# Every matmul of a convolution-and-token-mixing kernel as a 64 by 64 array quarter

## The chip, the cores and the metric

The kernel runs on one core of a Trainium2 chip. The metric is the device time of one execution in microseconds (us). Inputs and output are float32 in device memory; inside the core the matmul operands are bfloat16.

## The reference

There are eight batches of 4224 tokens with 192 features. A causal convolution with seven softmax-normalised taps, one set of taps for each of eight heads of 24 features, makes `y`; then a token mixer without softmax follows.

```python
w = softmax(weight, axis=-1)                       # 8 heads x 7 taps
y[b, s, h, :] = sum_k w[h, k] * x[b, s - 6 + k, h, :]
wq, wk = y @ w_q, y @ w_k                          # 192 -> 64
W_tok = (1 / 8) * einsum("bsd,btd->bst", wq, wk)
mixed = einsum("bst,btd->bsd", W_tok, y)
out = relu(mixed) @ w_out                          # 192 -> 192
```

Since nothing non-linear stands between `wq`, `wk` and `mixed`, the kernel never forms the 4224 by 4224 matrix. It uses mixed = wq (wk' y) / 8 and wk' y = w_k' (y' y), so that per batch it needs the Gram matrix y' y (192 by 192), a 64 by 192 matrix M = w_k' (y' y) / 8, and mixed = wq M.

## The kernel before, in words

Everything is unrolled. Each step is an object of class `Op` with the engines that may run it, its emitter, what it `needs`, and the accumulator (PSUM) banks that it fills or drains. `Planner.plan` reads a written-out order, the string `PLAN`: `118F4` is operation 118 on TensorE in full-array mode into bank 4, `A` is ScalarE, `D` VectorE, `G` GpSimd, `S` SyncE. `Program.place` then gives each engine its operations in that order and works out the semaphore waits. So the order on each queue, the engine that drains each bank, and the bank are set by hand in `PLAN`; there is no scheduler on the chip. Seven banks are dealt out to steps; bank 7 (`GB`) holds the Gram matrix.

Per batch the steps are these, with the lines that the profile names:

- Load (`gen_load`, L513): GpSimd issues DMAs that read x as float32 and write it as bfloat16 into `XW`. A chunk is 128 tokens, of which 122 are new: each chunk repeats the six tokens before it, so that the convolution of a chunk is one product with a 128 by 128 band matrix. `XW` holds all eight batches, and all loads are issued without waiting for the compute.
- Convolution (`gen_conv`): band matrix of one head times up to 18 chunks x 24 features, by `halves` either as one 128 by 128 matmul (L315) or as two 128 by 64 ones (L316, L317). ScalarE or VectorE copies the bank to `Y` as bfloat16 (L621).
- Turning `Y` (`gen_transpose` L321 to L323, `gen_transpose_hi` L678), drained by VectorE into `YTL` (L648) and `YTH` (L688).
- Queries (`gen_wq`, L707 and L711), drained into `WQT` (L728).
- Gram (`gen_gram`, L744): three matmuls per chunk with a 64-column weight, in the upper and lower half of the columns of the array.
- Weights of the mix (`gen_mix_weights`, L763, L807), and then per block of 512 + 512 tokens the mix (`gen_mix`, L836, L848, L856), a relu into `RT` (L873, L874), the product with `w_out` (`fin` L902, `fin_other` L920), the copy to `OUT` (L941) and the store by SyncE (L949).

The three ways of splitting the array are called `COL2` (two tiles of 128 rows by 64 columns), `ROW2` (64 by 128) and `FULL`. The second half of batch b (mix, product, store) is interleaved in `PLAN` with the first half of batch b + 1. The stationary operand of each matmul is loaded by an instruction of its own, so each matmul of the program is two instructions of TensorE (PE and PEld in the profile).

```python
# gen_load, a full part: n chunks of 128 tokens, 122 apart
XW[:, b, full[0] : full[0] + n, :],
bass.AP(x_t, base + (CW * full[0] - KC + 1) * D, [[D, 128], [CW * D, n], [1, D]]),
# gen_gram, one chunk
for p, r, z, o, st in ((0, 0, D, 0, begin), (64, 64, D, 64, begin), (64, LO, D, 0, False)):
    mm = e.matmul(bank(GB)[p : p + 64, o : o + z - r], Y[0:w, yb, c, r : r + 64], Y[0:w, yb, c, r:z], ...)
# halves, unless the mode is FULL
e.matmul(out[0:64], lhsT[:, 0:64], rhs, **k)
return e.matmul(out[64:128], lhsT[:, 64:128], rhs, **k)
```

Of the kernel before, what the change touches and what calls it, by code (L numbers as in the profile page):

```python
# [6 lines left out]
ALU = mybir.AluOpType  # L7
# [5 lines left out]

PLAN = """
1D 38G 2D 13G 37G 39G 40G 8D 19D 41G 42G 9D 56G 57G 14D 58G 59G 60G 61G 62G 63G 5D 64G 15P 65G 12D 66G 67G
68G 69G 70G 71G 72G 73G 74G 0S 22D 75G 20D 76G 77G 78G 23D 24D 25A 16P6 6D 79G 80G 21D 11D 81G 26D 27D 17P
4D 28D 18A 29D 30P5 7D 33P6 34D 35D 31A 32A 36P 84F4 85D 90F3 91A 88P1 89D 86P5 87A 116P5 142P 94P2 95D 92F1
93A 96F3 43S 98F6 99A 97D 118F4 117D 106F5 102F1 104F3 82G 100F6 143P 107D 144P 3D 105A 103A 101D 145P 83G
110F5 108F6 109A 112F3 113A 111D 119D 114F0 120F1 115A 126P2 127D 130P6 131D 47A 124F0 48A 125D 46A 44S
122F5 128P2 146P 10D 147P 121D 49A 140P4 53A 50A 132P0 123D 138P3 129D 134P2 141D 148A 149P6 52A 133A 159P4  # L20
157P0 150D 45S 51A 151F6 135A 139D 160A 155F2 158D 161F4 154A 153A 152A 222P6 136P0 162A 137A 211P1 156D
171P4 197P 54A 224A 167P2 168A 213D 165P5 172D 169P0 198P 170A 166D 221P3 210P5 163P0 199P 55A 173F2 223D
225P3 212A 217P5 164A 214P0 226P 174D 179F2 218F 180D 219D 215F 227A 177F2 178D 244F4 175F3 216A 220S 181P5
264P0 233P6 202P 176D 243P2 246A 265A 182D 228P4 232P0 245A 235D 229P 254P6 256A 201P 234A 262P2 230D 231S
185P6 186D 263A 268P4 266P0 267A 200P 255P6 269D 195P3 187P2 196A 203D 239P4 236P0 257D 258P6 240F 188A 241A
183P3 184D 204F2 205A 237F 259F 247P4 250P2 248F 251F 238A 242S 260D 261S 249A 270F0 271A 189P6 190A 304P
276P4 277A 274P0 206P6 252D 253S 272P2 305P 191P4 208A 207A 209A 328P5 275D 273A 317P0 192D 330A 288P2 289D
290P3 278P4 279D 193P5 194D 318F6 329F2 319A 286F0 340F1 280F4 320A 321P5 331A 291D 332P2 287D 342A 335P0
322P 323A 281D 333P 336P 337A 309P 292P4 284F5 334D 338S 324P2 339P0 361P6 363A 325F 293D 282F4 341A 351P6
285D 298P5 353A 326D 327S 373P0 371P2 283D 306P 374A 302P4 303A 294P6 295A 375P0 299D 372D 300P5 301D 369P2  # L30
296P4 297D 362P6 307P 376A 343P0 350P4 370A 346P2 344P 364A 385F6 347F 352A 345D 308P 310D 357P0 348A 349S
365P4 354P2 358P 386D 311F5 312D 355F 356D 359A 360S 387F6 388D 313F5 316A 315A 366F 377F0 383F2 314A 447P5
411P 425P6 378A 384D 379P0 380D 367A 368S 449A 381P3 427A 436P2 438D 412P 424P5 435P0 382A 397P3 395P4 398D
389F2 426A 428P5 396D 431P3 437A 429P 432P 458P0 390D 430A 414P 460A 457P1 459A 442P5 433D 434S 439P3 415P
440F 441A 443F 444D 445S 446P1 468P0 413P 476P3 482P5 470A 448A 399P0 393P1 416P 469P2 483A 417A 477D 400D
478F3 453P5 471A 479A 394D 450P0 418F2 419D 454F 455A 451F 480F3 391F2 409P5 452A 456S 481D 401P6 402A 464P0
461P3 465P 466A 472P6 462P 392D 403P2 410D 463D 467S 492P5 493D 488P0 489A 518P 490P3 404D 407P5 491A 484P0
408D 485D 405P2 486P3 487A 406D 520P 494P5 495D 420P1 421A 423A 506P0 504P2 502P3 422A 531P4 505D 473F 554F1
496F2 507D 543F0 474D 475S 503D 533A 497D 532F6 500F5 556A 519P 516P2 542P3 545A 534D 535P0 501D 538P5 536F
537A 517D 539F 565F2 567A 544D 546P3 549P0 547P 550P 575P2 577A 540D 541S 548D 585P5 508P2 551A 552S 564P3  # L40
586D 553P0 555A 509D 523P 587P5 588A 522P 589P0 590A 566D 521P 576P6 583P4 578A 560P2 557P0 524D 525F6 526D
561F 558F 527F6 584A 562A 498F5 530A 579P4 559D 563S 528A 571P2 568P0 572P 580P 529A 573A 569P 499D 514P5
515A 512P6 513A 570D 574S 591P2 593P0 594A 581D 582S 639P5 510P4 599P6 592D 511D 600D 638P2 640A 595P0 601P4
602D 596A 641A 625P 597P2 650P6 652A 627P 660P0 642P4 661F6 598D 607F2 605F3 606D 662A 608D 643P 644D 663A
649P0 651A 626P 609P6 645P2 656P0 653P4 610D 646P 647D 648S 657P 654P 682P6 655D 684D 630P 658A 659S 628P
694P2 695A 613P0 603P1 683P6 690P4 691A 696P2 614D 611P0 629P 685A 604D 623P1 697A 692P4 693A 672P6 612D
617P0 615P3 624D 674D 671P1 618A 664P5 686P4 631D 632F0 616D 673A 665F 666A 706F3 633D 634F0 637A 687P 688A
689S 675P1 667P5 635A 707D 678P3 676P 636A 668P 669D 670S 679P 757P0 759D 732P 677A 702P1 700P5 680A 681S
701D 746P3 748A 619P0 620D 734P 756P3 758D 703A 745P5 733P 698P0 621P2 708P3 709D 747A 704P5 699A 622A 768P4
760P0 705A 752P2 761P 762A 770D 749P5 753P 710F4 711D 750F 779F1 781D 714P0 715D 754A 736P 720P2 763P3 778P0  # L50
751A 755S 767P5 780A 721D 764P 789P2 737P 791D 769D 735P 801P0 716P2 765A 766S 730P3 797P5 738D 718P4 731D
717D 790P3 802A 739P0 719D 712P1 713D 722P2 723D 798A 792A 740A 799P5 800A 803P3 771P0 793P2 772P 773A 774P5
804D 775P 782P3 776A 777S 785P0 783P 794P 795D 796S 786P 805P5 839P 784A 726P2 809P3 806D 787A 788S 811P0
810A 727D 724P5 813P6 814D 812A 807P3 728P2 815P0 816D 808A 725A 741P1 742A 821P6 822D 825P3 826D 823P4 744A
743A 853P1 729A 864P0 866A 852P5 854A 863P2 824D 855D 840P 875P0 877A 841P 827P4 859P5 865D 867P2 856P0 868P
860P 869A 857P 828D 886P4 861D 842P 870P2 874P5 858A 862S 876A 871P 896P0 897P1 888D 843P 817P4 885P5 872D
873S 878P2 898A 899A 881P0 879P 818D 837P4 838D 844P 887A 880A 819P6 829P5 845D 846P2 847A 892P3 820D 882P
900P6 893P 830D 831P2 848P5 883A 884S 833P0 832A 851A 901P 849A 894D 889P1 850A 904P4 906A 890P 905P3 907A
834D 917P0 902D 903S 835P6 891D 895S 928P4 930A 919D 908P2 916P0 909P 910A 911S 836D 929F6 931A 912P4 918D
913P 924P0 914A 915S 920P2 925P 926A 927S 941F6 943D 921F 932P4 953P0 955D 952P6 933P 922A 923S 940P2 942A  # L60
936P0 954D 937P 956P6 957P 934D 935S 944P2 945F 948P4 949P 938A 939S 958D 959S 946A 947S 950A 951S
""".split()

COL2, ROW2, FULL = "128x64", "64x128", "128x128"


class Op:


    n = 0  # L70

    def __init__(self, engines, emit, ns, needs=(), after=(), banks=0, drains=None, vt=0.0, mode=COL2, tail=0.0, whole=False):
        self.engines = (engines,) if isinstance(engines, str) else tuple(engines)
        self.emit = emit

        self.ns = ns
# [7 lines left out]
        self.vt = vt  # L84
        self.mode = mode

        self.whole = whole
        self.tail = tail
        self.users = 0
        self.bank = None  # L90
        self.engine = None
        self.end = None

        self.lands = 0.0

        self.size = 0
        Op.n += 1
        self.id = Op.n


class Planner:

    ENGINES = {"P": "PE", "F": "PE", "A": "ACT", "D": "DVE", "G": "POOL", "S": "SP"}

    def __init__(self, nbank):
        self.ops = []
        self.order = []
        self.nbank = nbank
# [8 lines left out]
    def plan(self):  # L117
        drains = {}
        for op in self.ops:
            if op.drains is not None:  # L120
                drains.setdefault(op.drains.number, []).append(op)
        users = [[] for _ in range(self.nbank)]
        place = {}
        for turn in PLAN:
            number, engine, bank = re.fullmatch(r"(\d+)([PFADGS])(\d*)", turn).groups()
            op = self.ops[int(number)]
            op.engine = self.ENGINES[engine]
            if engine == "F":
                assert op.whole
                op.mode = FULL  # L130
            assert op.engine in op.engines and op.number not in place
            if op.banks:
                op.bank = int(bank)
                for i in range(op.bank, op.bank + op.banks):
                    op.needs += users[i]
                    users[i] = drains[op.number]
            assert all(x.number in place for x in op.needs + op.after)
            place[op.number] = len(self.order)
            self.order.append(op)
# [892 lines left out]
```

## Time and profile before

| what | value |
|---|---|
| runs of the kernel before | 169.85, 170.89 and 171.77 us, median 170.89 |
| span of the profiled execution, first to last instruction | 168.6 us |
| TensorE (PE) busy | 158.3 us, 2874 matmuls |
| weight loads (PEld) | 116.1 us, 2882 |
| ScalarE (ACT), VectorE (DVE) | 123.8 us in 207, 116.2 us in 201 |
| granted TensorE clock | 0.994 |
| device memory read and written | 27.56 MB and 25.95 MB |

The profiled execution's own time is not listed beside its span; the three timed runs lie 1.3 to 3.2 us above that span, and their median 2.3 us. Busy time of TensorE counts a matmul until its modelled end, so that several matmuls overlap in it; weight loads run beside matmuls. A line such as `L744 PE MATMUL ps<-y 122*64 122x192` is a matmul with a weight of 122 rows by 64 columns that streams 192 columns. The shares of the DMA queues are of the time of 16 engines; two packets in flight on one engine count twice, so that they can add to more than 100%.

### The profile page before, as it was taken

What the parts mean: (1) busy time and instruction counts of PE and PEld (TensorE: products, weight loads), DVE (VectorE), ACT (ScalarE), POOL (GpSimd) and SP (SyncE); (2) the same over time, 40 slices, a digit from 0 to 9 for tenths busy, and PEclk for the clock granted to TensorE, in tenths of its full rate; (3) what the DMA queues carried; (4) which work ended last, traced back from release to release, by engine and by line L of the source; (5) the groups of instructions that cost most, each with busy time, mean ns of one, the idle gap of its engine ahead of it and who ended that gap; (6) DMA issues with size and microseconds to landing.
All of it is one profiled execution on the core that took longest, in us unless ns stands there. A gap on an engine that the chain in (4) does not pass through costs nothing.

```text
span 168.6 us, 6398 instructions
## 1 busy us (share of the span) xinstructions
PE 158.3 (94%) x2874; PEld 116.1 (69%) x2882; DVE 116.2 (69%) x201; ACT 123.8 (73%) x207; POOL 30.3 (18%) x39
## 2 busy tenths in 40 slices
PE   6978999999999999999999999999999999999980
PEld 1458846876677886777865867787778777884640
DVE  5745878774678777566999686875957758578640
ACT  3233699798977869888566978578897889568970
POOL 7999553530503120000000000000000000000000
PEclk9999999999999999999999999999999999999997
DMA  2999999999999999999999999996644463095897
GB/s 23 172 190 185 205 191 196 189 241 301 263 328 208 300 268 276 299 251 317 284 287 199 289 282 341 235 273 232 231 176 190 189 257 149 0 368 218 315 363 283
DMA packets 48154, 40.31 MB, mean 239 GB/s; under 512 B 37632, under 2 KB 40960, under 8 KB 48128
## 3 DMA queue, kind: packets, MB, share of 16 engines
q0 software_dynamic: 36128, 13.61, 67.6%
q1 hardware_dynamic: 12000, 26.31, 43.1%
q8 instruction: 22, 0.36, 0.8%
q14 instruction: 4, 0.03, 0.1%
HBM read 27.56 MB, written 25.95 MB: 317 GB/s over the span
## 4 chain that ended last, share of the span: by engine, by line
PE 78%; ACT 8%; DMA 4%; DVE 3%; issue 2%; POOL 1%; POOLq 0%; ACTq 0%
PE ps L744 14%; PE ps L902 12%; PE ps L920 9%; PE ps L316 8%; PE ps L321 5%; PE ps L836 5%; DMA out_dram<-out_sb 4%; PE ps L678 4%; PE ps L707 4%; ACT y L621 4%; PE ps L711 3%; PE ps L856 3%; PE ps L315 3%; PE ps L322 3%; PE ps L317 2%
## 5 line engine op out<-in xcount | busy, mean ns | idle before, releaser
L621 ACT CAST y<-ps 122x864 bf16<-122x864 f32 (+3 forms) x48 | 37.2, 794 | 11.6 <-PE ps L315 5.8
L873 ACT ACTIVATE rt<-ps 128x1024 bf16<-128x1024 f32 (+3 forms) x56 | 38.7, 725 | 8.3 <-PE ps L836 6.8
L941 ACT COPY out_sb<-ps 128x768 f32<-128x768 f32 (+1 forms) x43 | 32.6, 779 | 11.9 <-PE ps L920 11.3
L513 POOL DMA_DIRECT2D xw<-in_x_dram x34 | 29.9, 909 | 29.4 <-issue 28.6
L941 DVE COPY out_sb<-ps 128x768 f32<-128x768 f32 (+1 forms) x29 | 23.9, 831 | 14.0 <-PE ps L920 12.7
L744 PEld LDWEIGHTS ps<-y 122*64 122x64 bf16 x840 | 29.4, 110 | 5.3 <-issue 2.2
L744 PE MATMUL ps<-y 122*64 122x64 bf16 (+3 forms) x840 | 32.8, 221 | 0.1
L648 DVE COPY ytl<-ps 128x976 bf16<-128x976 bf16 (+1 forms) x40 | 23.3, 592 | 7.2 <-PE ps L321 4.1
L621 DVE CAST y<-ps 122x816 bf16<-122x816 f32 (+3 forms) x24 | 21.5, 902 | 8.1 <-PE ps L317 5.4
L316 PE MATMUL ps<-xw,band 128*64 128x408 bf16 (+2 forms) x104 | 24.9, 342 | 0.0
L317 PE MATMUL ps<-xw,band 128*64 128x408 bf16 (+2 forms) x104 | 24.9, 342 | 0.0
L920 PE MATMUL ps<-wol,rt 64*128 64x192 bf16 (+1 forms) x264 | 23.9, 248 | 0.4
L902 PE MATMUL ps<-woh,rt 64*128 64x192 bf16 x264 | 22.4, 250 | 0.8 <-ACT out_sb L941 0.3
L874 DVE TENSOR_SCALAR rt<-ps 128x512 bf16<-128x512 f32 (+3 forms) x24 | 18.0, 755 | 3.1 <-PE ps L848 1.4
L920 PEld LDWEIGHTS ps<-wol,rt 64*128 64x128 bf16 (+1 forms) x264 | 15.2, 113 | 5.0 <-PE ps L902 2.5
L902 PEld LDWEIGHTS ps<-woh,rt 64*128 64x128 bf16 x264 | 11.7, 114 | 6.8 <-issue 1.8
L728 DVE CAST wqt<-ps 128x512 bf16<-128x512 f32 (+1 forms) x24 | 14.0, 583 | 2.8 <-PE ps L711 2.5
L688 DVE COPY yth<-ps 128x732 bf16<-128x732 bf16 x24 | 12.5, 534 | 4.5 <-PE ps L678 4.2
L902 PE MATMUL ps<-wol,rt 64*128 64x192 bf16 x177 | 15.4, 243 | 0.0
L711 PE MATMUL ps<-yth,wqh 128*64 128x512 bf16 (+1 forms) x72 | 14.9, 361 | 0.0
L707 PE MATMUL ps<-ytl,wql 128*64 128x512 bf16 (+1 forms) x72 | 14.5, 367 | 0.0
L321 PE MATMUL ps<-ident,y 122*128 122x122 bf16 (+1 forms) x159 | 12.0, 217 | 0.9 <-ACT y L621 0.7
(117 smaller groups left out, 209.8 us busy)
## 6 DMA issues: line engine op xcount, KB each, us to landing
out_dram<-out_sb SPq DMA_DIRECT2D x28, 768.0 KB, 7.3
xw<-in_x_dram POOLq DMA_DIRECT2D x7, 816.0 KB, 40.3
xw<-in_x_dram POOLq DMA_DIRECT2D x7, 768.0 KB, 42.9
out_dram<-out_sb SPq DMA_DIRECT2D x8, 384.0 KB, 3.1
xw<-in_x_dram POOLq DMA_DIRECT2D x2, 432.0 KB, 7.3
out_dram<-out_sb SPq DMA_DIRECT2D x8, 96.0 KB, 5.1
xw<-in_x_dram POOLq DMA_DIRECT2D x1, 384.0 KB, 5.1
xw<-in_x_dram POOLq DMA_DIRECT2D x8, 45.8 KB, 28.0
```

What stands on the lines that cost most here:

```text
L316: e.matmul(out[0:64], lhsT[:, 0:64], rhs, **k)
L317: return e.matmul(out[64:128], lhsT[:, 64:128], rhs, **k)
L321: return e.transpose(out, in_, identity)
L513: lambda e, op, part=part: e.dma_start(*part),
L621: return e.copy(dst, src) if op.engine == "ACT" else e.tensor_copy(dst, src)
L648: lambda e, op: e.tensor_copy(YTL[:, t0:t1], bank(mm_l.bank).bitcast(BF16)[:, 0:cols]),
L707: last = e.matmul(ps[64 * i : 64 * i + DH, 0:n], WQL[:, :], YTL[:, starts[i] : starts[i] + n], start=True, stop=False)
L744: mm = e.matmul(bank(GB)[p : p + 64, o : o + z - r], Y[0:w, yb, c, r : r + 64], Y[0:w, yb, c, r:z], start=st, stop=end, skip_group_check=True,
L873: return e.activation(dst, src(), AF.Relu)
L902: last = e.matmul(bank(op.bank + a)[:, (i - q) * D : (i - q) * D + D], RT[p, slot, a if lo else 2, i:n:nt], WOL[p, :] if lo else WOH[p, :] ...
L920: last = e.matmul(bank(fh.bank + a)[:, (i - q) * D : (i - q) * D + D], RT[p, slot, a, i:n:nt], WOL[p, :], start=False, stop=True, skip_gro ...
L941: return e.copy(dst, src) if op.engine == "ACT" else e.tensor_copy(dst, src)
```

## The change

The whole kernel is rewritten around pieces of 64 tokens.

- Every matmul has a weight of 64 rows by 64 columns, at one of four places of the array (row half r, column half c); four such matmuls stand next to each other in the order. Only the run-up matmuls on zeros and one turn at the start use the full array.
- A batch is two halves of 33 pieces of 64 tokens; the first half stands in partitions 0 to 63 and the second in 64 to 127. x is loaded without overlap. The convolution of a piece is a band matrix on the piece (`BANDM`) plus one on the piece before it (`BANDP`).
- `XW` holds four batches instead of eight (`NX = 4`), so a load waits until the convolution of four batches earlier has read its place. The first batch is loaded by 17 DMAs, each later one by 5.
- The Gram matrix has one accumulator bank for each row half. ScalarE or VectorE copies the first to `G0F`, and VectorE adds the second to it.
- All eight banks are dealt out. A step that fills two banks names them singly, and each is drained by an operation of its own, on either engine; a `w` in `PLAN` marks a drain of both by one operation.
- Where two row halves must add into one bank, the product is in two steps (`fin_a` and `fin_b`, `wq_a` and `wq_b`, `m_a` and `m_b`) and the second waits for the first to end.
- `OUT` has eight places instead of four. The stores of the last batch are not split in two.
- A new `PLAN`. The program has 6512 matmuls where it had 2882.

The diff, cut to its core:

```diff
-    XW = sbuf("xw", [128, B, NCC, D], BF16)
+    XW = sbuf("xw", [128, NX, 1 + NW, D], BF16)
...
-                bass.AP(x_t, base + (CW * full[0] - KC + 1) * D, [[D, 128], [CW * D, n], [1, D]]),
+                    lambda e, op, r=r, j=j, n=n: e.dma_start(
+                        XW[rows(r), slot, 1 + j : 1 + j + n, :],
+                        bass.AP(x_t, (b * S + r * HALF + T * j) * D, [[D, T], [T * D, n], [1, D]]),
+                    ),
...
+                    for k, band in ((1, BANDM), (0, BANDP)):
+                        for r in range(2):
+                            for c in range(2):
+                                j = 16 * q + NS * c + s0 + k
+                                last = e.matmul(
+                                    two(op.bank)[rows(c), r, i * W : i * W + W],
+                                    band[rows(r), h, :],
+                                    XW[rows(r), slot, j : j + n, GRP * h : GRP * h + GRP],
...
+                    for k in range(2):
+                        for c in range(2):
+                            last = e.transpose(
+                                ps[rows(k), c, o : o + T],
+                                Y[rows(c), yb, slots(q, r) + s, T * k : T * k + T],
+                                IDENT[rows(c), rows(c)],
+                            )
...
-                for p, r, z, o, st in ((0, 0, D, 0, begin), (64, 64, D, 64, begin), (64, LO, D, 0, False)):
-                    mm = e.matmul(
-                        bank(GB)[p : p + 64, o : o + z - r],
-                        Y[0:w, yb, c, r : r + 64],
-                        Y[0:w, yb, c, r:z],
+                for o, a, z, st, k in ((0, 0, D, begin, 0), (T, T, D, begin, 1), (0, 2 * T, D, False, 1)):
+                    for c in range(2):
+                        if s == NS and c == 0:
+                            continue
+                        y = Y[rows(c), yb, slots(q, r) + s, :]
+                        g = first.bank if first else op.bank
+                        last = e.matmul(
+                            two(g)[rows(k), c, o : o + z - a], y[:, a : a + T], y[:, a:z],
...
+        g0 = add(both, copy(lambda op: G0F[:, :], lambda op: bank(first.bank)[:, 0:D]), "g0",
+            needs=grams, drains=first, writes=[g0f_place])
+        g1 = add("DVE",
+            lambda e, op: e.tensor_tensor(GSB[:, :], bank(first.bank, 1)[:, 0:D], G0F[:, :], ALU.add), "g1",
...
+                for i in (i0, i0 + 1):
+                    o = (i - i0) * D
+                    for t in range(2):
+                        for r in range(2):
+                            last = e.matmul(
+                                two(op.bank)[rows(t), r, o : o + D], RTH[rows(r), hi, c, some(t, i)], WOH[rows(r), :],
+                                start=i == i0, stop=False, skip_group_check=True)
```

More of the change, by code (lines that the diff above doesn't have):

```diff
@@ L140, in plan @@
-        assert len(self.order) == len(self.ops)
+                    users[i] = drains.get((op.number, k), [op])
+            if whole or op.banks == 2 and any(x.half is None for x in drained[op.number]):
+                x = op.drains if whole else op
+                assert x.bank[1] == x.bank[0] + 1
+            if whole:
+                op.whole = op.twin
+                op.needs += op.twin.needs
+                op.twin.within = op
+                placed.add(op.twin.number)
+            assert all(x.number in placed for x in [*op.needs, *op.after, *op.apart])
@@ L365, in bass_lightweight_conv__then__hypermixer_token_mlp_kernel @@
-    zero_m = add("DVE", lambda e, op: e.memset(MBD[:, :, :], 0.0), 200, vt=-8.5)
+            for _ in range(n):
+                last = e.matmul(bank(op.bank)[:, 0:512], RUNUP[:, 0:128], RUNUP[:, :], start=True, stop=True)
+            return last
+        return add("PE", emit, f"run_up{n}", needs=needs, after=after, banks=1)
     ident = add(
@@ L465, in spread, with band_p @@
             return last
-        fill = add("PE", spread, 215, needs=[taps, stept], after=[run_2, *fills], banks=1)
+        fill = add("PE", spread, "spread", needs=[taps, stept], after=[run_2, *fills], banks=1)
         fills.append(fill)
+        def band_p(e, op, half=half, fill=fill):
+            dst = BANDP[:, 4 * half : 4 * half + 4, 0:16]
+            src = bank(fill.bank)[:, 256:320].rearrange("p (i h) -> p h i", h=4)
+            return e.copy(dst, src) if op.engine == "ACT" else e.tensor_copy(dst, src)
@@ L821, in gen_mix @@
[L821 to L842 removed]
+                        ps[rows(r if k == 2 else k), o : o + T],
@@ L891, in gen_mix @@
-        pieces = 2 if b == B - 1 and nt > 1 else 1
-        step = 2 if nt > 1 else 1
-        for q in range(0, nt, step):
-            iq = range(q, q + step)
-            def fin(e, op, iq=iq, q=q):
+            for k in range(2):
+                r = 1 - k
+                last = e.matmul(
+                    two(qa.bank)[0:T, r, 0:T], WQL[rows(k), :], YTX[rows(k), T * r : T * r + T],
+                    start=False, stop=True, skip_group_check=True)
+            return last
+        qa = add("PE", begin, "wqx_a", needs=casts_q, reads=[ytx_place], banks=2)
@@ L955, in gen_mix @@
-        rt_read[n_rt - 1] = readers
-        store_of[n_out - 1] = stores
-    later = []
+                for i in (i0, i0 + 1):
+                    o = (i - i0) * D
+                    for t in range(2):
+                        for k in range(2):
+                            r = 1 - k
+                            last = e.matmul(
+                                two(fa.bank)[rows(t), r, o : o + D], RTL[rows(k), lo[r], c, some(t, i)], WOL[rows(k), :],
+                                start=False, stop=True, skip_group_check=True)
```

1215 lines of the change are left out of this document (626 added, 589 removed).

## The prediction

> **What bounds the kernel now.** I read the page's busy times and slices first, then the matmul rows by form, the starts of single matmuls in the timeline, and last the DMA queues and short stretches of the DMA engines.
>
> ```profile
> PE 158.3 (94%) x2874; PEld 116.1 (69%) x2882; DVE 116.2 (69%) x201; ACT 123.8 (73%) x207; POOL 30.3 (18%) x39
> ...
> PE   6978999999999999999999999999999999999980
> ...
> DMA  2999999999999999999999999996644463095897
> ```
>
> TensorE is full from the third slice to the last but one; ScalarE and VectorE are not. A busy TensorE may still wait, so I looked at starts. In the timeline at 60.25 us, 192-column matmuls of one tile start 83 ns apart, 64-column ones 29 ns, 122-column turns 53 ns, 512-column ones 0.21 us: columns at 2.4 per ns and 2.5 to 5 ns more.
>
> ```profile
> 60.25 0.71 PE L744 MATMUL ps<-y 122*64 122x192 bf16 x18
> 60.89 0.36 PE L902 MATMUL ps<-woh,rt 64*128 64x192 bf16 x4
> ```
>
> By that rate the starts of the whole trace add up to 136.3 us of streaming, 13.8 us in 114 changes of tile shape (mostly 94 ns; 125 ns between the last start of L744 and the first of L902 above), 13.5 us of other waits (5.9 us of it in the first 20 us) and 4.9 us after the last matmul: 168.5 of the span of 168.6. So TensorE bounds it now.
>
> Second reading, the DMA engines:
>
> ```profile
> q0 software_dynamic: 36128, 13.61, 67.6%
> q1 hardware_dynamic: 12000, 26.31, 43.1%
> q8 instruction: 22, 0.36, 0.8%
> ```
> ```profile
> 20.00:30.00 10.00, 9.89 (x163) 6.19 (x157) 7.75 (x12) 9.13 (x19) 3.72 (x5) 1.00 1.60 193
> 70.00:80.00 10.00, 10.00 (x182) 7.37 (x176) 5.69 (x10) 8.54 (x14) 0.00 (x0) 1.00 1.33 276
> 130.90:131.40 0.50, 0.50 (x24) 0.50 (x20) 0.50 (x2) 0.50 (x2) 0.00 (x0) 1.00 0.95 381
> 141.50:142.10 0.60, 0.60 (x8) 0.14 (x6) 0.60 (x2) 0.45 (x1) 0.00 (x0) 1.00 0.06 26
> 142.20:143.00 0.80, 0.80 (x27) 0.72 (x27) 0.80 (x1) 0.80 (x2) 0.00 (x0) 1.00 0.00 0
> ```
>
> The last two columns are the share of the 16 DMA engines and GB/s written. q8 is TensorE's own instructions: 22 pieces of 16 KB for 5764 instructions, one for every 262. A fetch takes 0.8% x 16 x 168.6 / 22 = 0.98 us (single packets 0.88 to 1.42, median 0.95).
>
> Two things are to be seen. First, the price of data. From 20 to 30 us there are only loads: 193 GB/s / 384 bytes is 503 rows of x per us, over 16 engines. From 130.9 to 131.4 us only stores: 381 / 0.95 = 401 GB/s. From 70 to 80 us the packets are 2607 rows and 1.74 MB of stores: 5.2 + 4.3 = 9.5 us of 10, so the two prices add. Second, one engine does the fetches besides its sixteenth of the data. At 141.5 us a single engine (0.06 = 1/16) is still working off its share of a store, at 26 GB/s, while 15 have ended; the fetch at 142.12 follows. In packets counted by time, 16 stores are in flight at 130.1, 15 from 131.0 to 131.5 (fetch to 131.48), then 16 again; likewise 15 at 149.3 to 149.9, 153.7 to 154.4. Among loads the mean falls from 22.6 to 21.3 in flight during a fetch, nine tenths of one engine's part. Of the 16 landings of each late store 15 come together and one 1 to 1.9 us later.
>
> So that engine's day before: 35,424 rows / 503 = 70.4 us, stores 25.95 MB / 401 = 64.7, weights 0.9, fetches 22 x 0.98 = 21.6: 157.6 us. It can work from the first x packet (3.0 us) to the last landing (167.8), 164.8 us; the trace has no packet in flight for 8.0 us in between. It is the second-tightest thing in the kernel, 7 us from the bound, and nothing on the page's queue shares says so, because they are means over 16 engines.
>
> **The change part by part.**
>
> TensorE's columns, per batch, four tiles together (columns of a group of four, not of each): convolution 16 x (192 + 216) = 6528 (before 6720); Gram 33 x 87 ns = 2.87 us (before 35); turns 48 groups of 64 columns at 29 ns = 1.4 us (before 53 of 122 columns at 53 ns = 2.8); queries 6 x 0.216 = 1.3 (before 8); mix 6 x 0.216 = 1.3 (before 8); product 48 x 82.5 ns = 4.0 (the same). With 0.1 to 0.4 us for each left-over piece: 14.4 us per batch, 115 in all, and some 6 us at the start: 121 against 136.3. The changes of shape go, but for one or two: -13.6. That four quarters run side by side the trace shows once, in the run-up:
>
> ```profile
> L345 PE MATMUL ps<-runup 64*64 64x512 bf16 x12 | 1.9, 631 | 0.0
> ```
>
> Four start within 10 ns and the next four 0.43 us later, at half clock; one after another the twelve would take 5.1 us. So TensorE alone would gain 29 us: 168.6 to about 140.
>
> Drains. ScalarE's copies last 801 ns for 768 columns, 600 for 512, 521 for 432, 320 for 192; VectorE's 956, 684, 606, 353, and 661 for 976 bf16. Where one follows another without a wait it starts 110 ns (ScalarE) or 85 ns (VectorE) before the former ends. The built program gives ScalarE 271 operations (118 of 384 to 432 columns, 67 of 512 as the main kinds) and VectorE 259. At those prices ScalarE is occupied 115 us (before 111), VectorE 118 (before 107). More operations, as banks are drained singly; no bound by itself.
>
> Start. The first convolution needs five DMAs on GpSimd's queue instead of two, with the identity (L369, 0.31 us) behind the first two instead of the first. An issue there takes 0.55 to 1.0 us by size: I take 0.65, so the identity and all that follows it (step, turn, taps, bands) is 0.7 us later, and the last of the 17 issues of batch 0 ends at about 12.7 us instead of 7.2. The last pieces land at 15 us; TensorE by then has 6.6 of its 8.8 us done, so the price is some 3 us where TensorE bounds it, and nothing where the DMA engine does.
>
> The second steps (`fin_b`, `wq_b`, `m_b`): 0.25 us each if nothing stands between (L920 waited 2.5 us in 10 times), and in the new order another step mostly does. The Gram sum adds one 192-column operation (0.35 us) per batch on the way to the mix, behind which only the mix of that batch waits; other batches' work covers it. Four places of `XW`: a load waits for the convolution of four batches ago, long done. I take 0 to 3 us for all of these.
>
> x without overlap: 33,840 rows instead of 35,424, 67.3 us instead of 70.4 on every engine. Stores 64.7 as before. The eight places of `OUT` allow two batches to wait.
>
> Instructions. 6512 matmuls with a weight load each are 13,024 instructions; at 262 to a piece, 50 fetches instead of 22. Nothing hides them: the engine that does them had 7 us left. At 0.95 us they take 47.5 us, 26 more (at nine tenths of that 43, at 0.98 49; with their longest row, 1.42, 71). Its sum: 67.3 + 64.7 + 0.9 + 47.5 = 180.4 us. Every load and every store is spread over all 16 engines and is complete when the last has landed, so neither the next convolution nor the reuse of `OUT` can go past it. This engine becomes the bound: 22.5 us per batch, against 14.4 for TensorE.
>
> Sum: first x packet 3.0 + 180.4 + 0.8 from the last landing + 1 us without work = 185 us of span, and 2.3 to the median of the runs: 187.
>
> **The rivals.**
>
> A, the fetches find gaps. The 15 other engines need only 132.9 us. If the fetches took nothing from the data, compute decides. In the Gram stretch of a batch TensorE needs 5.9 us and each draining engine 3.8; in the rest TensorE 8.5 and the drains 10.4: 16.3 us a batch. Start 10.5 + 130.5 + 5 + 2.3 = 148. This is the case on the other side; it decides if a fetch costs the data less than (148 - 2.3 - 3.8 - 132.9) / 50 = 0.2 us. For it: TensorE never waited for a fetch in the kernel before. Against it: the 15 in flight. The Trainium skill (Runtime: NRT & Kernel Launch, section Instruction fetch mechanics) holds that crossing a 16 KiB block costs one bump of a queue's tail, mostly hidden, as the sequencer dispatches more slowly than the fetch fills. By that rule the time is A's; the trace agrees as to TensorE, but it shows a data engine held for 0.95 us at each block.
>
> B, TensorE cannot issue that many. The densest long stretch before, 83.5 to 85.1 us, has 71 matmuls and 65 loads, 11.8 ns for each, and the array was full there, so the limit lies below. At 11.8 ns, 13,024 take 153.7 us; with 7.8 before the first convolution, 4.9 and 2.3: 169, and 172 with the 3 us of the later start.
>
> C, A's conditions, but the drains pack badly, as banks come in pairs and the Gram holds two: 8 x 17.8 + 17.8 = 160.
>
> That the quarters run in turn, two at a time, would be 230 us of streaming; L345 excludes it.
>
> **How the numbers follow.** The forecast has 70%, A 15%, C 7%, B 8%. The forecast's own range is 178 to 195 (43 to 49 us of fetches, up to 5 us of idle time). The range of 156 to 196 leaves out A and the tail of the forecast. A measurement of this kernel tells about 1% from no change. Faster is A and C, 22%; within 1% is most of B, 5%; slower is the forecast and the rest of B, 73%.
>
> **What would show it.** Right: about 50 packets and 0.8 MB in q8; TensorE idle before L656 (convolution) with a DMA of `xw` as releaser, or drains waiting for stores; the mean share of DMA engines lower than before with one engine always at work; streaming without changes of shape; 22 us per batch. The step on the fetches is wrong if TensorE stays above nine tenths and the last landing comes along with the other 15; that on TensorE is wrong if 192-column matmuls of one tile start more than 90 ns apart without a wait.

## Result, and the profile after

The changed kernel takes 264.0 us (median of 4 runs, 262.2 to 264.9) where the kernel before, beside it on the same chip, takes 170.5 us (169.9 to 171.8): a ratio of 1.547, with an interval of 1.537 to 1.557. The forecast was 187 us, 156 to 196. The sign was right and the size wrong: 16 us more were forecast, and 93 came. In the profiled executions TensorE's mean granted clock is 0.857, where it was 0.994.

The page of the changed kernel, engines and slices:

```profile
span 260.1 us, 13937 instructions
...
PE 168.2 (65%) x6512; PEld 141.1 (54%) x6512; DVE 127.4 (49%) x257; ACT 127.1 (49%) x269; POOL 39.0 (15%) x57
...
PE   5746367652985668644995668557957697399840
...
PEclk9977657798698879995698899979997889959995
DMA  6999999949349890799318301830084006602786
```

TensorE is busy for 65% instead of 94%, and seldom full for long. The draining engines are down to 49%. The DMA engines have whole slices with nothing to do. So no engine is the bound, and something that none of these rows counts as work sets the time. The DMA queues:

```profile
q0 software_dynamic: 34752, 13.00, 43.2%
q1 hardware_dynamic: 11120, 26.33, 27.4%
q8 instruction: 51, 0.84, 1.3%
```

51 pieces of TensorE's instructions, as forecast (50). But if the engine that fetches them were the bound, it would always be at work. By the trace's packets no packet of any queue is in flight for some 68 us, and exactly one for another 28. The chain that ended last and the list of waits name the rest:

```profile
PE 56%; issue 29%; DVE 4%; ACT 4%; POOL 2%; DMA 1%; DVEq 0%; POOLq 0%
```
```profile
PEld ps L776 <- issue: 30.8, 18, 4.5
...
PE ps L776 <- issue: 27.3, 12, 4.4
PEld ps L698 <- issue: 22.8, 10, 3.8
```

"issue" is time in which TensorE waits for nothing that the profile shows: 29% of 260 us is 75 us, most of it at L776 (Gram) and L698 (turns), the lines with the most instructions per us. I numbered TensorE's instructions in the trace. The waits lie at numbers 449, 705, 961 and so on: 37 of the 51 places that are 256 instructions apart have one of over 0.5 us, 83.2 us together (counted from the last start of a matmul, less the streaming of its columns; some 75 us from the end that the profile models). 256 instructions are one piece of 16 KB, called a block below. A stretch table of one such block, cut where it starts, where the fetch of the next begins and lands, and where the next starts; the columns are length, PE, PEld, DVE, ACT and POOL busy with counts, clock, DMA share and GB/s:

```profile
148.92:150.02 1.10, 1.10 (x102) 1.10 (x105) 0.39 (x1) 0.00 (x0) 0.00 (x0) 1.00 0.00 0
150.02:150.97 0.95, 0.79 (x39) 0.65 (x29) 0.95 (x3) 0.27 (x1) 0.00 (x0) 1.00 0.06 17
150.97:152.23 1.26, 0.00 (x0) 0.00 (x0) 0.65 (x2) 0.33 (x1) 0.00 (x0) 1.00 0.00 0
```

The fetch (0.06 is one DMA engine of 16; 17 GB/s for 0.95 us is 16 KB) begins 1.10 us after the block before it has begun, with the DMA engines empty. TensorE runs out 0.8 us later, and starts again 1.26 us after the landing: 3.31 us from block to block, of which 1.65 lie between the last start of a matmul and the next. While x is loaded it is worse, because the fetch begins later:

```profile
20.00:30.00 10.00, 5.66 (x223) 4.75 (x227) 2.81 (x8) 3.39 (x11) 5.68 (x8) 0.75 1.59 190
70.00:80.00 10.00, 8.25 (x360) 7.08 (x349) 7.92 (x17) 7.97 (x19) 0.00 (x0) 1.00 0.47 171
```

From 20 to 30 us, with the DMA engines at 1.59, TensorE is idle for 4.3 of 10 us (before: 0.1), and its granted clock is 0.75 (before: 1.00). Blocks take 6 to 7 us there.

In the words of the prediction's account: streaming 141.6 us (before 136.3), changes of shape 0.8 (13.8), waits at block boundaries 83.2 (none over 0.5 us), other waits 24.7 (13.5), after the last matmul 9.9 (4.9): 260.2.

### The profile page after: what moved, and what is told of

It is laid out like the page before. It is cut to its first block, busy times and chain, and to the rows that moved or that the text cites. A ratio compares the mean times of both kernels' runs of the same rounds, so it can differ in the third digit from the quotient of the medians.

```text
span 260.1 us, 13937 instructions
## 1 busy us (share of the span) xinstructions
PE 168.2 (65%) x6512; PEld 141.1 (54%) x6512; DVE 127.4 (49%) x257; ACT 127.1 (49%) x269; POOL 39.0 (15%) x57
## 4 chain that ended last, share of the span: by engine, by line
PE 56%; issue 29%; DVE 4%; ACT 4%; POOL 2%; DMA 1%; DVEq 0%; POOLq 0%
PE ps L776 14%; PE ps L656 10%; PE ps L998 5%; PE ps L978 5%; PE ps L698 4%; PE ps L983 4%; PE ps L920 3%; PE ps L723 2%; DVE y L354 2%; PE ps L854 2%; POOL xw L555 2%; PE ps L937 2%; DVE out_sb L354 2%; PE ps L869 1%; DMA xw<-in_x_dram 1%
## 5 line engine op out<-in xcount | busy, mean ns | idle before, releaser
L776 PE MATMUL ps<-y 64*64 64x192 bf16 (+2 forms) x1584 | 45.4, 265 | 27.3 <-issue 27.3
L776 PEld LDWEIGHTS ps<-y 64*64 64x64 bf16 x1584 | 42.3, 137 | 31.4 <-issue 30.8
L354 ACT CAST y<-ps 128x432 bf16<-128x432 f32 (+5 forms) x78 | 38.3, 521 | 36.3 <-PE ps L656 34.1
L656 PE MATMUL ps<-xw,bandm 64*64 64x216 bf16 (+3 forms) x576 | 37.0, 268 | 9.4 <-issue 7.1
L354 DVE CAST y<-ps 128x384 bf16<-128x384 f32 (+5 forms) x51 | 26.3, 536 | 25.0 <-PE ps L656 24.8
L354 ACT COPY out_sb<-ps 128x384 f32<-128x384 f32 (+1 forms) x63 | 30.6, 504 | 14.6 <-PE ps L998 14.3
L656 PE MATMUL ps<-xw,bandp 64*64 64x216 bf16 (+3 forms) x576 | 36.6, 266 | 1.4 <-issue 1.4
L354 DVE COPY out_sb<-ps 128x384 f32<-128x384 f32 (+1 forms) x60 | 32.1, 559 | 10.3 <-PE ps L998 9.1
L978 PE MATMUL ps<-woh,rth 64*64 64x192 bf16 x512 | 30.1, 257 | 3.6 <-issue 2.5
L983 PE MATMUL ps<-wol,rtl 64*64 64x192 bf16 x512 | 29.7, 248 | 2.2 <-issue 2.2
L656 PEld LDWEIGHTS ps<-xw,bandm 64*64 64x64 bf16 x576 | 23.8, 120 | 12.9 <-issue 9.2
L698 PE MATMUL ps<-ident,y 64*64 64x64 bf16 x1024 | 15.1, 204 | 21.6 <-issue 21.6
L698 PEld LDWEIGHTS ps<-ident,y 64*64 64x64 bf16 x1024 | 13.4, 116 | 23.3 <-issue 22.8
L656 PEld LDWEIGHTS ps<-xw,bandp 64*64 64x64 bf16 x576 | 24.1, 121 | 2.1 <-issue 1.9
L998 PE MATMUL ps<-wol,rtl 64*64 64x192 bf16 x512 | 23.7, 257 | 1.2 <-issue 0.8
```

The lines of the kernel that those rows point to most:

```text
L354: return e.copy(dst(op), src(op)) if op.engine == "ACT" else e.tensor_copy(dst(op), src(op))
L656: last = e.matmul(two(op.bank)[rows(c), r, i * W : i * W + W], band[rows(r), h, :], XW[rows(r), slot, j : j + n, GRP * h : GRP * h + GRP], ...
L698: last = e.transpose(ps[rows(k), c, o : o + T], Y[rows(c), yb, slots(q, r) + s, T * k : T * k + T], IDENT[rows(c), rows(c)],)
L776: last = e.matmul(two(g)[rows(k), c, o : o + z - a], y[:, a : a + T], y[:, a:z], start=st, stop=end, skip_group_check=True,)
L978: last = e.matmul(two(op.bank)[rows(t), r, o : o + D], RTH[rows(r), hi, c, some(t, i)], WOH[rows(r), :], start=i == i0, stop=False, skip_g ...
L983: last = e.matmul(two(op.bank)[rows(t), r, o : o + D], RTL[rows(r), lo[r], c, some(t, i)], WOL[rows(r), :], start=False, stop=False, skip_ ...
```

## The experiments

Three theories stood against each other. T1: a round trip. The next block is fetched only when the one before has begun, and can't run until some 1.4 us after its landing; TensorE waits wherever 256 instructions take less than that. T2: the prediction's, a DMA engine that is full. T3: quarters are slow by themselves.

**More instructions in the kernel before.** Each Gram matmul in two halves of its columns (`b_gram_split`), and then the output projection as well (`b_gram_fin_split`):

```
-                    mm = e.matmul(bank(GB)[p : p + 64, o : o + z - r], Y[0:w, yb, c, r : r + 64], Y[0:w, yb, c, r:z], ...
+                    half = (z - r) // 2
+                    for u in range(2):
+                        mm = e.matmul(bank(GB)[p : p + 64, o + u * half : o + u * half + half], ...
```

> The kernel before, with each Gram matmul issued as two halves of its columns: the same columns, banks, order and tile shapes, but 704 matmuls (1408 instructions, 5.5 blocks of 256) more, 7444 instructions in all. Theory T1 (round trip): the fetch of one block of 256 TensorE instructions starts only after the block before the last has been used up, and the first instruction of the block runs 1.2 to 1.6 us after its landing, so a block can't pass in less than about 3.5 us with quiet DMA engines and 5 to 7 us while transfers fill them. The kernel before passes a block in 7.2 us on average and waits for none, but has come near the limit at places. T1 expects 180 to 185 us, with waits of TensorE exactly at boundaries of 256 instructions. T2 (the prediction's: the one DMA engine that fetches is the bound, 0.95 us a fetch on top of its share of the data): 5.5 more fetches, 171 to 175 us. T3 (what costs is the quarters themselves: weight loads, clock, concurrent pieces): no quarter more is made here, so 170 to 173 us.

> As the run before, and also each output projection matmul (fin, fin_other) as two halves of its columns: 8854 instructions, 34.6 blocks, the same columns. T1: 195 to 205 us, waits at boundaries of 256 instructions in every batch. T2: 11 more fetches of 0.95 us on the fetching engine, 174 to 180 us. T3: 170 to 176 us.

Measured: 191.7 us, ratio 1.124 (1.118 to 1.131), and 202.2 us, ratio 1.185 (1.173 to 1.197). T2 and T3 are out as the whole cause: they allowed 175 and 180 at most. T1 had the first too low, and the second right for only half of the reason. In `b_gram_split` the waits at boundaries are 10.8 us, in `b_gram_fin_split` some 16 of the 32 us. Streaming is longer too, by 9.1 us in the first (145.4): in its trace Gram matmuls of 32 and of 64 columns on one tile start 32 ns apart alike, four to a chunk, so that a chunk takes 127 ns instead of 87. That part was missing in T1's number; with it, T2 would come to 184 at most, still short of 191.7. The longest waits of `b_gram_split` for "issue" are at the split line and at the turns:

```profile
PEld ps L746 <- issue: 4.6, 9, 1.7
PE ps L678 <- issue: 3.4, 3, 1.4
```

**The round trip by itself.** A small kernel of 768 groups of four quarter matmuls on the same data, 24 blocks, without loads and with all of x loaded by GpSimd:

```
for i in range(768):
    for r in range(2):
        for c in range(2):
            p = slice(64 * r, 64 * r + 64)
            e.matmul(PS[64 * c : 64 * c + 64, 512 * r : 512 * r + COLS], W[p, 0:64], W[p, 0:COLS], start=True, stop=True)
```

> A small kernel by itself: 768 groups of four 64 by 64 quarter matmuls of 64 columns, 6152 TensorE instructions or 24 blocks of 256, all on the same data, nothing else running; the output is one drained piece, not the reference's. T1: every block takes 3.3 to 3.6 us from boundary to boundary although its array work is only about 1 us: 75 to 90 us for the matmuls. T2: 24 fetches of 0.95 us one after the other, 23 to 28 us. T3: the quarters as fast as the array takes them, some 25 to 45 us without any boundary at 256.

> The same small kernel while GpSimd loads all eight batches of x (26 MB, some 67 us of the DMA engines by the loads of the kernel before). T1: a block takes 6 to 7 us while the loads run and 3.3 to 3.6 us after, so 110 to 150 us if the loads last as long as 67 us. T2: the loads plus 24 fetches, 90 to 100 us. T3: the matmuls are done in 25 to 45 us as in the quiet run, the loads end last at some 75 us.

Measured, one run each: 92.1 us and 121.8 us, T1 both times, if with slightly longer blocks than its 3.3 to 3.6 us. Quiet, every block after the first takes 3.45 to 4.00 us, 3.58 on average; one block of it, cut as above (columns as above, without ACT):

```profile
43.47:44.64 1.17, 1.17 (x89) 1.17 (x92) 0.00 (x0) 0.00 (x0) 0.50 0.00 0
44.64:45.59 0.95, 0.75 (x57) 0.61 (x48) 0.00 (x0) 0.00 (x0) 0.50 0.06 17
45.59:46.92 1.33, 0.00 (x1) 0.00 (x0) 0.00 (x0) 0.00 (x0) 0.50 0.00 0
```

The same three parts as in the kernel: 1.17 until the fetch begins, 0.95 for it, 1.33 until the block starts. With loads the blocks take 6.20 us, ten times in a row:

```profile
35.64:37.70 2.06, 1.92 (x128) 1.79 (x128) 0.00 (x0) 0.00 (x0) 0.50 1.60 193
37.70:39.40 1.70, 0.00 (x0) 0.00 (x0) 0.00 (x0) 0.00 (x0) 0.50 1.63 201
39.40:40.29 0.89, 0.00 (x0) 0.00 (x0) 0.00 (x0) 0.21 (x1) 0.50 1.51 181
40.29:41.83 1.54, 0.00 (x0) 0.00 (x0) 0.00 (x0) 1.54 (x2) 0.50 1.64 193
```

The fetch begins at 39.40, 3.76 us after the block instead of 1.1; its own time and what follows are as before. So what the loads cost is a wait ahead of the fetch, 2.7 us, not a slower fetch. The data is hardly slowed in turn: 181 GB/s during the fetch, 193 to 201 around it.

**Longer and shorter blocks.** The same instructions with 512 and with 128 columns in each, and with the full array in place of quarters:

```
 COLS = 64      ->  COLS = 512 with loads (m_long_loads);  COLS = 128 without (m_double)
-                    last = e.matmul(PS[64 * c : 64 * c + 64, 512 * r : 512 * r + COLS], W[p, 0:64], W[p, 0:COLS], ...)
+                last = e.matmul(PS[:, 512 * r : 512 * r + COLS], W[:, 0:128], W[:, 0:COLS], ...)      (m_full)
```

> The small kernel with all eight batches of x loaded, and 512 columns in each quarter matmul instead of 64: the same instructions and loads, eight times the columns. T1: a block now holds 32 groups of 512 columns, 6.8 us at the full clock, more than the 6.20 us of a round trip under loads: no wait at the boundaries once the clock is full, 165 to 180 us. If a fetch held TensorE up whatever the block contains, 6.8 + 1.8 to 4.5 us a block: 230 to 260 us.

> The small quiet kernel with 128 columns in each quarter matmul instead of 64: the same instructions, twice the array work (1.7 us a block at the full clock, twice that at the lowest one); the output is one drained piece, not the reference's. T1: the work of a block still fits under the round trip at the full clock and just does not at the low one: 3.5 to 4.5 us a block, 85 to 110 us. If the wait came on top of the array work, 1.8 us more for each of 24 blocks than in the run with 64 columns: 130 to 140 us.

> The small quiet kernel with each quarter matmul replaced by one over the full array (128 by 128, 64 columns): as many instructions, four times the array work; the output is one drained piece, not the reference's. T1: the array work of a block stays far below the round trip of its instructions, so the same 3.45 to 3.73 us a block and 90 to 95 us as with quarters. T3 (it is quarters that start slowly): no wait at the boundaries, and a different time.

Measured, one run each: 174.5, 94.2 and 97.4 us. With 512 columns a block holds 6.91 us of work, more than 6.20, and nothing waits:

```profile
36.65:43.56 6.91, 6.91 (x136) 3.54 (x130) 0.00 (x0) 2.27 (x2) 1.00 1.60 193
```

Eight times the columns cost 53 us over `m_loads`, and twice the columns 2 us over `m_quiet`: array work below the round trip is nearly free, and above it the fetch is. In `m_full` my arithmetic was off: 128 matmuls of 64 columns over the full array are 3.73 us a block, not far below the round trip but in its range of 3.45 to 4.00. No wait and another time is what T3 had said, so this run does not tell T1 from T3. TensorE is busy throughout; the run says only that a fetch that has 3.73 us is hidden here:

```profile
PE 92.0 (96%) x3076; PEld 90.7 (95%) x3076; DVE 0.6 (1%) x2; POOL 0.2 (0%) x4
```

**What the fetch waits for under loads.** The same bytes of x, laid out so that the engines move long pieces:

```
-                    bass.AP(x_t, (b * S + r * S // 2) * D, [[D, 64], [64 * D, 33], [1, D]]),
+                    bass.AP(x_t, (b * S + r * S // 2) * D, [[33 * D, 64], [D, 33], [1, D]]),
```

> The small kernel with the same bytes of x loaded, but 33 tokens in a row to each partition, so that the pieces that the DMA engines move can be longer than one token's 384 bytes. T1 says that a fetch waits for what is queued ahead of it in its engine, and leaves open what sets the 2.7 us of waiting: if it is a number of pieces, the wait grows or shrinks with their length (a block then takes 4 to 5 us or over 7 us while the loads run); if it is a stretch of time or of bytes, 6.2 us a block as with single tokens. T2 makes no difference between the two.

Measured, one run: 121.2 us, and blocks of 5.65 to 6.92 us, 6.3 on average while the loads run, though the pieces are now 12,672 bytes instead of 384. So it isn't a number of such pieces. Whether it is a time or a number of bytes, or where in the engine they stand, stays open.

**Less data in the changed kernel.** Loads cut, stores cut, both cut:

```
+                    ) if b >= NX else e.dma_start(          (loads of batches 4 to 7: 24 columns of one piece each)
...
-            dst = bass.AP(out_t, (b * S + 512 * (2 * q + c) + i0) * D, [[4 * D, 128], [HALF * D, 2], [1, n * D]])
+            dst = bass.AP(out_t, (b * S + 512 * (2 * q + c) + i0) * D, [[4 * D, 128], [1, GRP]])
```

> The changed kernel, with only the loads of batches 4 to 7 cut to 24 columns of one piece each (the places keep the data of four batches earlier); the stores are whole. T1 (round trip of a block of 256 TensorE instructions, longer while transfers fill the DMA engines): the loads ran until some 125 us; the blocks after the first loads take 3.5 to 4.5 us instead of 4 to 7, 235 to 250 us. T2 (bytes on the fetching engine): some 33 us of reading less, 225 to 235 us. T3 (quarters themselves): 255 to 265 us.

> The changed kernel, with only the large stores cut to 24 columns of one row group (most of the output isn't written); the loads are whole. T1: stores fill the DMA engines for some 60 of 260 us; the blocks that met them get 1 to 2 us shorter, 235 to 250 us. T2: 60 us of writing less on the fetching engine, 195 to 215 us. T3: 255 to 265 us.

> The changed kernel, with the loads of batches 4 to 7 cut to 24 columns of one piece each (the places keep the data of four batches earlier) and each of the large stores cut to 24 columns of one row group, so most of the output isn't written; TensorE's, VectorE's and ScalarE's work is all there. T1: from some 50 us on each block of 256 instructions passes in 3.3 to 3.8 us instead of 4 to 7: 200 to 215 us in all, still with a wait at every boundary. T2: with the data gone the fetching engine is free, the time falls to the work of TensorE and the drains, 145 to 160 us. T3: DMA has no part in it, 255 to 265 us.

Measured: 247.6, 243.7 and 227.2 us, that is 16, 20 and 37 us less than 264.0. The first two are in T1's ranges and outside T2's. In the third, half of the loads and nearly all of the stores are gone (9.0 MB moved instead of 40.2), no packet at all is in flight for half of the time, and the kernel is still 57 us slower than the one before. 38 boundaries still wait, 63.9 us together. T1 expected 200 to 215 for the last: it took every block at the quiet 3.3 to 3.8 us, but a block takes 4.15 on average, as the first batches are still loaded until 45 us and some blocks hold more work than a round trip.

**Fewer instructions in the changed kernel.** The Gram over 128 tokens, six blocks fewer:

```
-                    for c in range(2):
...
-                        y = Y[rows(c), yb, slots(q, r) + s, :]
+                    y = Y[:, yb, slots(q, r) + s, :] if whole else Y[rows(1), yb, slots(q, r) + s, :]
```

> The changed kernel, with the Gram matmuls over 128 tokens in 128 by 64 tiles instead of two 64 by 64 ones (even pieces to one accumulator bank, odd ones to the other): as many columns streamed (a pair of quarters side by side becomes one tile), 768 matmuls or 6 blocks of 256 instructions fewer. T1: 6 blocks fewer at 4 to 6 us, 225 to 245 us. T2 (fetching engine as the bound): 6 us less, 256 to 260 us. T3 (quarters themselves cost): the Gram's tile shape now changes against its neighbours 64 times at some 90 ns, 255 to 270 us.

Measured: 239.9 us, ratio to the kernel before 1.406 (1.393 to 1.419): 24 us for 6 blocks, 4 us a block, although 64 changes of shape come back (9.2 us in 67). T1 alone had that. Then everything put together that the same columns allow, in the order of the changed kernel:

```
-                                ps[rows(k), c, o : o + T], Y[rows(c), yb, slots(q, r) + s, T * k : T * k + T],
+                            ps[:, c, o : o + T], Y[rows(c), yb, slots(q, r) + s, 0 : 2 * T],
...
-                                two(op.bank)[rows(t), r, o : o + D], RTL[rows(r), lo[r], c, some(t, i)], WOL[rows(r), :],
+                            two(op.bank)[:, r, o : o + D], RTL[:, lo[r], c, some(i)], WOL[:, :],
```

> The changed kernel with its order, banks, loads and stores as they are, but quarters put together wherever the same columns can stream through a larger tile: Gram over 128 tokens (128 by 64), transposes of the lower 128 channels and the output projection over 128 weight columns (64 by 128), its lower part and that of the query projection over 128 rows, mixing of the lower channels in 64 by 128. 4000 matmuls or so, 31 blocks of 256 instructions instead of 51; TensorE changes tile shape some 200 times again (about 18 us by the 94 ns of the kernel before). T1: the first 16 to 18 blocks, while x is loaded, take 6.2 us, the others about 5 us of work: 175 to 195 us. T2 (fetching engine's bytes): 19 us less than the changed kernel, 240 to 248 us. T3 (the quarters themselves): most quarters are gone, 165 to 175 us with no waits at block boundaries.

Measured: 210.3 us in the run with the trace (217.4 in the other), 54 us less than the changed kernel, and more than T1 expected. There are 289 changes of shape, not 200, at 110 ns: 31.9 us instead of 18. And 13 boundaries still wait, 21.6 us. The instructions were traded for changes of shape. It beats neither `b_gram_fin_split`, which fetches more often (35 times against 32), nor the kernel before.

**The count alone.** Last, the kernel before with as many instructions as the changed one. A first try split the Gram in four and the projections in two:

> The kernel before with nearly as many TensorE instructions as the changed one: Gram matmuls in four parts of their columns, output projection and query projection in two, the same columns, tile shapes, order, banks, loads and stores; some 12,700 instructions, 49 to 50 blocks of 256 against 51. T1: 6.2 us a block until the loads end at some 95 us (15 blocks), then 3.5 to 4.5 us for the other 34 and 5 us at the end: 220 to 255 us, nearly the time of the changed kernel. If quarters, order, banks or the pieces of x have a large share in its 93 us, this kernel stays well below, 175 to 205 us. T2: 26 fetches more at 0.95 us on the fetching engine, 175 to 200 us.

Measured: 252.1 us, in T1's range, but for another reason in good part. Gram matmuls of 16 and of 32 columns on one tile start 32 ns apart alike; in the trace the split line takes over 70 us without its waits, where it took 23. Only 25.0 us are waits at boundaries. This run doesn't answer the question. A second one kept the parts at 64 to 128 columns; its cut shows the output projection:

```
-                                ... bank(op.bank + a)[:, (i - q) * D : (i - q) * D + D], ... WOL[p, :] if lo else WOH[p, :],
+                            for u in range(0, D, 64):
+                                ... bank(op.bank + a)[:, (i - q) * D + u : (i - q) * D + u + 64], ... (WOL if lo else WOH)[p, u : u + 64],
```

> The kernel before with as many TensorE instructions as the changed one, and no part under 64 columns but the last of a convolution: Gram and output projection in parts of 64 columns, query projection and mixing in parts of 128, convolution in parts of 96; the same columns, tile shapes, order, banks, loads and stores; 13,500 instructions, 53 blocks of 256 against 51.5. T1: 6.2 us a block until the loads end at some 95 us, then 3.5 to 4.5 us for the other 37, 5 us at the end: 230 to 265 us, with 60 us or more of waits at block boundaries. If quarters, order, banks or the pieces of x have a large share in the 93 us of the change: below 210 us. T2: 30 fetches more at 0.95 us, 178 to 200 us.

Measured: 259.5 us, ratio 1.525 (1.509 to 1.542). Its page and its chain look like those of the changed kernel:

```profile
PE 192.6 (74%) x6727; PEld 174.0 (67%) x6736; DVE 117.8 (46%) x201; ACT 126.2 (49%) x207; POOL 30.4 (12%) x39
```
```profile
PE 69%; issue 22%; ACT 3%; DMA 3%; POOL 1%; POOLq 0%
```

With the old order, banks, shapes and loads, 53 blocks take 89 us more than 23. The waits of over 0.3 us that end 1.1 to 1.75 us after a landing come to 57 us (85 in the changed kernel by the same count), just under what T1 asked for. The other 32 of the 89 us lie between the boundaries, 17 of them in streaming; they come with the splitting too, but not by the round trip. So a loss nearly as large as the changed kernel's can be had by the number of instructions alone. That the changed order, banks and pieces of x cost nothing is not shown: by the sums at the end of the section on the result, other waits grew by 11.2 us and the time after the last matmul by 5.0.

## Why the prediction was wrong

What bounded the kernel before. TensorE, and that stands. But the sentence on which rival A was weighed, that TensorE never waited for a fetch, was read as if there were room. The trace of before has the warning: its blocks took 5.3 to 8.2 us, the fetches began 3.1 to 4.0 us after the block while x was loaded, and at 109.6 us the first instruction of a block came 1.36 us after its landing, no later than in the blocks that wait now. The kernel before runs at the edge of the round trip.

The step that failed is the one on the instructions: "Nothing hides them: the engine that does them had 7 us left. At 0.95 us they take 47.5 us, 26 more". Number and price of the fetches were right (51, median 0.96 us). What was wrong is who pays. The sum gave them to a DMA engine that must also move its sixteenth of the data, 180 us in all, and put TensorE's own wait for a fetch at nothing. In the trace no engine at all has a packet for a quarter of the time, and TensorE pays, with 1.1 us before the fetch (3.8 under loads) and 1.3 after it, which the 0.95 did not hold: 83.2 us of waits at 37 boundaries, where the forecast had 26 us of work more on one DMA engine. By the windows above 51 blocks at 3.45 to 6.2 us are 176 to 316 us; the mean was 4.77. That the sign came out right is in part luck: fetches did cost the time, as said, but not in the way that gave 187.

Rival A, the fetches find gaps: they did, for the data, and the time was still not A's, because a fetch that costs the data nothing can cost TensorE 1.65 us. The Trainium skill (Runtime: NRT & Kernel Launch, section Instruction fetch mechanics) calls the crossing mostly hidden, since dispatch is slower than the fill. Where 256 instructions take over 3.45 us with quiet DMA engines, or over 6.2 us under loads, the runs agree (`m_full`, `m_long_loads`); in this kernel's Gram and turns they can take as little as 1.5 to 1.9 us, and the crossings are the largest part of what the change lost. The same section has the next block fetched while the current one runs, and speaks of only two blocks held, though it also gives TensorE room for 2048 instructions. The runs agree with two: even where nothing waits (`m_full`), the fetch of the next block begins 0.3 to 0.8 us after a block has begun, never earlier.

Rival B, TensorE cannot issue that many, at 11.8 ns for each: excluded. `m_quiet` issues 256 in 1.04 us at the full clock, 4.1 ns each, and in 1.68 at half. Rival C can't be told: the drains are at 49%.

TensorE's columns. That quarters run side by side and the shapes stop changing came as said (13.8 to 0.8 us). The 121 us did not: 141.6. The Gram took 22 ns per matmul outside the waits, 34.5 us instead of 23; with less data (`a_little_dma`) 17.7. What the sum left out is the granted clock. Two stretches of the changed kernel with nothing but Gram, both with full DMA engines; the columns are length, PE and PEld busy with counts (of L776 alone), clock, DMA share and GB/s:

```profile
58.03:58.73 0.70, 0.70 (x49) 0.70 (x50) 1.00 1.51 180
64.23:65.50 1.27, 1.27 (x47) 1.27 (x45) 0.50 1.60 193
```

At the full clock that is 14 ns a matmul, as forecast (87 ns for six); at half, 27. The clock is at half for 77 of the 260 us, and more than half of the Gram's matmuls fall there. Taken line by line, matmuls at half clock start some 19 us later in all than the same lines do at full clock, nearly all of the 20.6 us that were missing. Why the clock falls is not settled.

What would show it. Some 50 packets and 0.84 MB in q8 came, and streaming without changes of shape. One engine always at work did not; TensorE waited once before L656 for `xw`, 0.9 us at the start, and no drain waited for a store. Those rows drop the theory by themselves. The late sixteenth landing, read as the mark of the fetching engine, is there in both kernels: the last landing of a store of `OUT` comes 0.3 us or more after the other 15 in 28 of 32 stores (at most 1.85 us), and before in 25 of 44 (at most 1.79), though not in the last nine there. With more than twice the fetches the longest lag is hardly longer, and nothing waited for it, so it does not show an engine that has fallen behind.

## What to carry to other kernels

Count TensorE's instructions, two for each matmul, and set each stretch of 256 against the 3.5 us, or 6 us with full DMA engines, that these runs had: what ran shorter mostly waited, and the profile showed it as "issue" on the chain. A change that makes matmuls smaller for the array's sake must gain more than that. Columns added beneath the limit were nearly free (2 us for twice the columns), and instructions added beneath it cost about the whole round trip (4 us a block). When a trace shows no wait for a resource, look for the smallest distance to one before giving it no price.

## What the runs showed of the hardware

- Blocks that wait come 3.45, 3.73 or 4.00 us apart in the quiet small kernel, steps of 0.28 us, at half clock and nearly full clock (0.975 in `m_double`) alike. The round trip doesn't go with TensorE's clock.
- In `m_quiet` the granted clock falls to half at 11.5 us, after blocks in which TensorE was idle for 1.6 and 2.2 us, and stays there for 80 us with 1.5 to 2.3 us idle in each block (mean 0.565). With twice the columns (`m_double`) it is idle for 0.8 to 2.0 us in each block, and the clock stays near full (0.975).
- Gram matmuls of the changed kernel start 14 ns apart at the full clock and 27 ns at half, with the DMA engines full both times.
- Loads of x into bf16 in pieces of 12,672 bytes end only some 8 us sooner than in pieces of 384 bytes (the last piece begins at 66 against 74 us, one run each).
- On one tile, Gram matmuls of 16 and of 32 columns start 32 ns apart (`b_many`), and so do those of 32 and 64 (`b_gram_split`): no sooner than one of 64 columns in the kernel before (29 ns).
